# Gated linear recurrence and gated unit: when GpSimd issues the transfers of two weight matrices

## The chip, the cores and the metric

The kernel runs on one core of a Trainium2 chip. A core has five engines that each work through a queue of their own in order: PE (matrix multiplies, transposes and, counted apart, weight loads), DVE (VectorE), ACT (ScalarE), POOL (GpSimd) and SP, which here only issues transfers. DMA engines, 16 to a core, move data between HBM and the on-chip memory; SP, ACT and POOL can hand them work. The metric is device time in microseconds for one execution; lower is better. Time before is the median of five executions.

## The reference

Inputs are x, r_gate and i_gate of 4 x 6336 x 256 float32, a vector a_param of 256, two 256 x 256 weight matrices (w_val, w_out) and a convolution kernel conv_w of 5 x 256. Cut to what is computed:

```python
log_a = 8 * sigmoid(r_gate) * log(clip(sigmoid(a_param), 1e-6, 1 - 1e-6))
a_t   = exp(log_a)
gated = sqrt(max(1 - a_t * a_t, 1e-6)) * sigmoid(i_gate) * x
h_t   = a_t[:, t] * h + gated[:, t]          # recurrence over t, y[:, t] = h_t
gate  = sigmoid(sum_k conv_w[k] * y[t - 4 + k])   # causal, five taps
out   = (gate * (y @ w_val)) @ w_out
```

The two weight matrices are needed only in the last line, after the recurrence.

## The kernel before

The 4 x 6336 time steps are laid out as one row of 25,344 and cut into tiles of 512 steps (three of them 256), and tiles into chunks: one of 256, one of 512, 23 of 1024 (two tiles each), then 512, 256, 256. The channels are two halves of 128. Numbers below count tiles (g), chunk halves (k = 2 x chunk + half), and pieces of 256 output rows (q).

Per tile or chunk half these steps run, named as in the code:

- SP loads a tile of both gates (`load`, line 262, into `ri`) and of x (`loadx`, line 269, into `xt`).
- ACT takes tanh of both gates (`tanh`, line 354). The sigmoid is written through tanh.
- PE transposes the r half to channels (`srT`, line 379), ACT takes exp to get a (`exp`, line 388, into `aring`), POOL squares a (`e`, line 396, into `ering`).
- For a group of chunks at once (`UNITS`, the first two groups have chunks 0 and 1, and chunk 2), ACT takes the square root (`sq`, line 400). It needs another activation table, so a table load of 1.28 us goes before it and another after it.
- DVE or POOL makes (1 + tanh) * x (`u2`, line 365 on DVE, lines 369 and 370 on POOL), PE transposes the root to rows (`nT`, line 410), DVE multiplies (`xg`, line 417), PE transposes the product to channels (`xT`, line 426).
- DVE runs the recurrence (`scan`, line 444, into `yring`), PE the convolution (`conv`, line 470), ACT its tanh (`tg`, line 478), PE the product with w_val (`val`, line 486), DVE the gating (`gv`, line 496), PE the product with w_out (`out`, line 508), DVE or ACT the copy out (`osb`), SP the store.

The order in which each engine takes its steps is written out by hand (`ORDER`, line 48), a letter for a step. ACT starts with tanh 0, exp 0, exp 1, tanh 1, exp 2, tanh 2, tanh 3, exp 3, 4 and 5, tanh 4, and then both roots; POOL starts with six squares, e 0 to e 5, and then u2 of tile 2. A planner (`make_plan`) merges the five orders by estimated start times into one list, `plan`, and the steps are emitted in that list's order. Each engine keeps its own order; semaphores do the rest.

Ahead of the plan stands a setup: the small vectors, the identity matrices, the ten diagonal matrices of the convolution (`diag`, line 323, on DVE), the first eight load steps on SP, and the weights. `wv` (line 288) and `wo` (line 294) are bfloat16 tiles on chip; the matrices in HBM are float32, and the transfer converts them. POOL issues these transfers: four for `wv` (line 292, one for each half of rows and of columns) and two for `wo` (line 296). In POOL's queue they stand behind the making of the identity matrix and ahead of e 0. The first readers are `val` of tile 0 and `out` of piece 0 on PE.

Of the kernel before, what the change touches and what calls it, by code (L numbers as in the profile page):

```python
# [9 lines left out]
P = 128  # L10
# [50 lines left out]
BANK_ORDER = ("2220300232032030101322321213031230312121301103230301320123103021230121321321012121032312030131032110"  # L61
              "3203210321303123021032021023120103120130231030231023013203121032031230131302102302031031220131201321"
              "03120202310233203213201203302132002310232320202312303203031210")
TABLE, SEM, DMA_LAT = 1.3, 0.15, 2.2
START, ACT_START = 0.9, 4.6
FP32 = mybir.dt.float32
# [158 lines left out]
def kernel(  # L225
# [11 lines left out]
    nc = tc.nc  # L237
    B, S, D = x.shape
    assert D == 2 * P, f"kernel assumes D == 256, got {D}"
    H = D // P  # L240
# [31 lines left out]
    with tc.manual_schedule():  # L272
# [13 lines left out]
        b025 = const.tile([P, 1], FP32, name="b025")  # L286
        nc.vector.memset(b025[:], 0.25)
        wv = const.tile([P, H, D], BF16, name="wv")

        for hk in range(H):  # L290
            for m in range(H):
                nc.gpsimd.dma_start(wv[:, hk, m * P:(m + 1) * P].rearrange("p (h c) -> p h c", h=H),
                                    moe_w_val[hk * P:(hk + 1) * P, :].rearrange("p (h m c) -> p m h c", h=H, m=2)[:, m])
        wo = const.tile([P, H, D], BF16, name="wo")
        for h in range(H):
            nc.gpsimd.dma_start(wo[64 * h:64 * h + 64, :, :],
                                moe_w_out[h * P:(h + 1) * P, :].rearrange("(m c) n -> c m n", m=2))
        khf = const.tile([P, H], FP32, name="khf")
        wcol = const.tile([P, H, CONV_K], FP32, name="wcol")
        with tc.tile_pool(name="ps_setup", bufs=1, space=bass.MemoryType.PSUM) as ps_setup:  # L300
# [222 lines left out]
        def op_store(g, eng):  # L523
# [2 lines left out]
            nc.sync.dma_start(of[t0:t0 + nt, :].rearrange("(p j) d -> p j d", j=nj),  # L526
                              live.pop(("osb", g))[:, 0:nj, :])

        ops_by_name = dict(load=op_load, loadx=op_loadx, tanh=op_tanh, u2=op_u2, srT=op_srT, exp=op_exp, e=op_e, sq=op_sq,
                           nT=op_nT, xg=op_xg, xT=op_xT, scan=op_scan, conv=op_conv, tg=op_tg, val=op_val, gv=op_gv,  # L530
                           out=op_out, osb=op_osb, store=op_store)
        for (t, op, i, eng, dur) in plan:
            ops_by_name[op](i, eng)


# [28 lines left out]
```

## Time and profile before

| | before |
|---|---|
| median of five executions | 313.71 us (311.72 to 314.97) |
| the profiled execution | 314.52 us, of it 312.7 us span from the first instruction to the last |
| busy ACT | 284.5 us (91% of the span) |
| busy DVE | 269.7 us (86%) |
| busy PE | 252.1 us (81%); weight loads 163.3 us (52%) |
| busy POOL | 245.3 us (78%) |
| moved by DMA | 104.51 MB in 30,797 packets, 334 GB/s over the span |
| mean granted PE clock | 0.965 |

How to read it: no engine is busy all the time, and the largest share, ACT's, leaves 28 us of the span idle. A step's price is therefore not its busy time; it is what it adds to the chain of waits that ends last. The page's slices cut the span in 40 parts of 7.8 us. The timeline lists instructions by start time with, in brackets, the idle time of the engine before them and what ended it. A transfer issued by POOL shows on POOL's row for as long as GpSimd prepares it; the data lands later.

### The profile page before, as it was taken

What the parts mean: (1) busy time and instruction counts of PE and PEld (TensorE: products, weight loads), DVE (VectorE), ACT (ScalarE), POOL (GpSimd) and SP (SyncE); (2) the same over time, 40 slices, a digit from 0 to 9 for tenths busy, and PEclk for the clock granted to TensorE, in tenths of its full rate; (3) what the DMA queues carried; (4) which work ended last, traced back from release to release, by engine and by line L of the source; (5) the groups of instructions that cost most, each with busy time, mean ns of one, the idle gap of its engine ahead of it and who ended that gap; (6) DMA issues with size and microseconds to landing.
All of it is one profiled execution on the core that took longest, in us unless ns stands there. A gap on an engine that the chain in (4) does not pass through costs nothing.

```text
span 312.7 us, 6602 instructions
## 1 busy us (share of the span) xinstructions
PE 252.1 (81%) x2591; PEld 163.3 (52%) x2591; DVE 269.7 (86%) x273; ACT 284.5 (91%) x224; POOL 245.3 (78%) x154
## 2 busy tenths in 40 slices
PE   1226765887799987996897889979899989999994
PEld 1114533554565654655654565647555755666562
DVE  3015898698999989999799899999999999998983
ACT  5899898599999999999999979999999999989544
POOL 6273699859998997899999989998997987986000
PEclk9999987799999998899899899999999999999998
DMA  8999999996999699999994999999979979843345
GB/s 239 357 403 410 411 408 308 392 330 205 373 417 412 280 326 415 419 358 374 421 413 170 335 418 414 374 376 389 414 245 376 414 301 310 321 138 159 136 192 214
DMA packets 30797, 104.51 MB, mean 334 GB/s; under 512 B 4391, under 2 KB 4654, under 8 KB 30766
## 3 DMA queue, kind: packets, MB, share of 16 engines
q1 hardware_dynamic: 29376, 103.82, 87.2%
q0 software_dynamic: 1376, 0.26, 1.0%
q8 instruction: 20, 0.33, 0.4%
q14 instruction: 11, 0.09, 0.1%
q10 hardware_dynamic: 14, 0.01, 0.0%
HBM read 78.39 MB, written 25.95 MB: 334 GB/s over the span
## 4 chain that ended last, share of the span: by engine, by line
ACT 27%; DVE 25%; PE 22%; issue 13%; DMA 9%; SPq 3%; DVEq 0%; ACTq 0%
ACT tring L354 10%; DVE yring L444 10%; DMA ri<-in_i_gate_dram 9%; PE gp L470 6%; ACT ering L400 6%; ACT aring L388 5%; DVE osb L519 5%; DVE gv L496 4%; PE bank L410 4%; PE val L486 4%; PE bank L508 4%; ACT tg L478 3%; DVE uring L365 3%; DVE uring L417 3%; PE bank L426 3%
## 5 line engine op out<-in xcount | busy, mean ns | idle before, releaser
L396 POOL TENSOR_TENSOR ering<-aring 128x1024 f32<-128x1024 f32 (+2 forms) x56 | 95.5, 1720 | 34.9 <-ACT aring L388 34.9
L444 DVE TENSOR_TENSOR_SCAN yring<-aring,yring,bank 128x1024 bf16<-128x1024 f32 (+5 forms) x54 | 110.4, 2054 | 3.8 <-PE bank L426 3.7
L370 POOL TENSOR_TENSOR uring<-t,xt 128x1024 bf16<-128x1024 f32 (+1 forms) x43 | 101.1, 2350 | 4.2 <-DMA xt<-in_x_dram 0.7
L354 ACT ACTIVATE tring<-ri 128x2048 bf16<-128x2048 f32 (+1 forms) x51 | 94.3, 1865 | 0.8 <-DMA ri<-in_i_gate_dram 0.6
L470 PE MATMUL gp<-yring,diag 64*64 64x512 bf16 (+15 forms) x1196 | 68.7, 358 | 5.1 <-ACT tg L478 4.7
L388 ACT ACTIVATE aring<-bank,khf 128x1024 f32<-128x1024 bf16 (+2 forms) x56 | 61.0, 1113 | 9.8 <-PE bank L379 9.2
L508 PE MATMUL bank<-wo,gv 128*128 128x256 bf16 x396 | 58.2, 276 | 11.1 <-DVE osb L519 4.2
L496 DVE SCALAR_TENSOR_TENSOR gv<-tg,val 128x1024 bf16<-128x1024 bf16 (+1 forms) x54 | 60.6, 1127 | 6.2 <-PE val L486 4.3
L478 ACT ACTIVATE tg<-gp 128x1024 bf16<-128x1024 f32 (+1 forms) x51 | 51.2, 1004 | 8.9 <-PE gp L470 8.3
L486 PE MATMUL val<-yring,wv 128*128 128x512 bf16 (+1 forms) x204 | 52.8, 382 | 0.9 <-DVE gv L496 0.8
L508 PEld LDWEIGHTS <-gv 128*128 128x128 bf16 x396 | 37.1, 99 | 31.1 <-issue 16.9
L519 DVE TENSOR_SCALAR osb<-bank 128x512 f32<-128x512 f32 x74 | 48.8, 680 | 2.6 <-PE bank L508 2.1
L379 PE MATMUL bank<-ident_b,tring 128*128 128x128 bf16 x396 | 34.9, 235 | 17.4 <-ACT tring L354 11.2
L470 PEld LDWEIGHTS <-diag 64*64 64x64 bf16 x1196 | 31.2, 110 | 30.7 <-issue 16.2
L369 POOL TENSOR_SCALAR t<-tring 128x1024 f32<-128x1024 bf16 (+1 forms) x43 | 45.1, 1048 | 2.0
L400 ACT ACTIVATE ering<-ering,b 128x2048 bf16<-128x2048 f32 (+3 forms) x15 | 46.3, 3108 | 0.1
L410 PE MATMUL bank<-ident_f,ering 128*128 128x128 f32 x198 | 35.2, 309 | 12.6 <-ACT ering L400 8.0
L379 PEld LDWEIGHTS <-tring 128*128 128x128 bf16 x396 | 28.4, 105 | 25.9 <-ACT tring L354 13.2
L417 DVE TENSOR_TENSOR uring<-bank,uring 128x1024 bf16<-128x1024 bf16 (+1 forms) x51 | 33.3, 666 | 7.1 <-PE bank L410 6.9
L426 PE MATMUL bank<-ident_f,uring 128*128 128x128 f32 x198 | 33.5, 292 | 6.3 <-DVE uring L417 4.6
L410 PEld LDWEIGHTS bank<-ident_f,ering 128*128 128x128 f32 x198 | 28.2, 207 | 19.8 <-ACT ering L400 10.7
L365 DVE SCALAR_TENSOR_TENSOR uring<-tring,xt 128x512 bf16<-128x512 bf16 x15 | 20.0, 1378 | 15.1 <-DMA xt<-in_x_dram 15.1
(32 smaller groups left out, 104.5 us busy)
## 6 DMA issues: line engine op xcount, KB each, us to landing
ri<-in_r_gate_dram SPq DMA_DIRECT2D x48, 512.0 KB, 8.7
ri<-in_i_gate_dram SPq DMA_DIRECT2D x48, 512.0 KB, 9.6
xt<-in_x_dram SPq DMA_DIRECT2D x48, 512.0 KB, 9.2
out_dram<-osb SPq DMA_DIRECT2D x48, 512.0 KB, 5.0
ri<-in_r_gate_dram SPq DMA_DIRECT2D x3, 256.0 KB, 5.5
ri<-in_i_gate_dram SPq DMA_DIRECT2D x3, 256.0 KB, 5.5
xt<-in_x_dram SPq DMA_DIRECT2D x3, 256.0 KB, 4.5
out_dram<-osb SPq DMA_DIRECT2D x3, 256.0 KB, 2.4
```

Of the source, the lines that this page charges most:

```text
L354: nc.scalar.activation(out=tring[:, r:i + 1:i - r, 0:nj, :], in_=ri[:, :, 0:nj, :], func=ACT.Tanh, scale=0.5)
L370: nc.gpsimd.tensor_tensor(out=u.rearrange("p w d e -> p w e d"), in0=t1.rearrange("p (w e) d -> p w e d", e=2), in1=xt.rearrange("p (w e) ...
L388: nc.scalar.activation(out=aring[:, h, a0:a0 + nt].rearrange("c (w p j) -> c w p j", p=P, j=nj), in_=live.pop(("srT", k))[:, 0:nt].rearran ...
L396: nc.gpsimd.tensor_tensor(out=ering[:, H * e0 + h * nt:H * e0 + (h + 1) * nt], in0=a, in1=a, op=ALU.mult)
L400: nc.scalar.activation(out=nring[:, 2 * H * e0:2 * H * e0 + H * m], in_=ering[:, H * e0:H * (e0 + m)], func=ACT.Sqrt, scale=-0.25, bias=b0 ...
L410: nc.tensor.transpose(out=nT[:, w * D + h * P:w * D + (h + 1) * P], in_=ering[:, n0 + w:n0 + nw * P:nw], identity=ident_f[:])
L444: nc.vector.tensor_tensor_scan(out=yring[:, h, y0 + c0:y0 + c1], data0=aring[:, h, a0 + c0:a0 + c1], data1=xT[:, c0:c1], initial=0.0 if fr ...
L470: nc.tensor.matmul(out=gp[64 * h:64 * h + 64, m, c0:c1], lhsT=diag[rows, h, kk, rows], rhs=yring[rows, h, src:src + c1 - c0], start=(sh == 0),
L486: nc.tensor.matmul(out=val[:, m, 0:nt], lhsT=wv[:, hk, m * P:(m + 1) * P], rhs=yring[:, hk, y0:y0 + nt], start=(hk == 0), stop=(hk == H - 1))
L496: nc.vector.scalar_tensor_tensor(out=gv[:, 0:nj, hs, :].rearrange("c j h p -> c j (h p)"), in0=tg[:, hs, 0:nt].rearrange("c h (p j) -> c j ...
L508: nc.tensor.matmul(out=ops[:, e * D:(e + 1) * D], lhsT=gv[:, 2 * i + e, hk, :], rhs=wo[:, hk, :], start=(hk == 0), stop=(hk == H - 1))
L519: nc.vector.tensor_scalar(out=dst, in0=ops[:], scalar1=0.5, scalar2=None, op0=ALU.mult)
```

## The change

The two loops that issue the six weight transfers move from the setup into a function, and the loop over the plan calls it once, right after it has emitted step ("e", 1). In POOL's queue the six transfers then stand between e 1 and e 2. Their sizes, shapes and order among themselves stay, the tiles `wv` and `wo` stay where they were allocated, and every other instruction keeps its place on its engine and its waits.

```diff
+WEIGHTS_AFTER = ("e", 1)
...
         wv = const.tile([P, H, D], BF16, name="wv")
-
-        for hk in range(H):
-            for m in range(H):
-                nc.gpsimd.dma_start(wv[:, hk, m * P:(m + 1) * P].rearrange("p (h c) -> p h c", h=H),
-                                    moe_w_val[hk * P:(hk + 1) * P, :].rearrange("p (h m c) -> p m h c", h=H, m=2)[:, m])
         wo = const.tile([P, H, D], BF16, name="wo")
-        for h in range(H):
-            nc.gpsimd.dma_start(wo[64 * h:64 * h + 64, :, :],
-                                moe_w_out[h * P:(h + 1) * P, :].rearrange("(m c) n -> c m n", m=2))
...
+        def load_weights():
+
+            for hk in range(H):
+                for m in range(H):
+                    nc.gpsimd.dma_start(wv[:, hk, m * P:(m + 1) * P].rearrange("p (h c) -> p h c", h=H),
+                                        moe_w_val[hk * P:(hk + 1) * P, :].rearrange("p (h m c) -> p m h c", h=H, m=2)[:, m])
+            for h in range(H):
+                nc.gpsimd.dma_start(wo[64 * h:64 * h + 64, :, :],
+                                    moe_w_out[h * P:(h + 1) * P, :].rearrange("(m c) n -> c m n", m=2))
...
         for (t, op, i, eng, dur) in plan:
             ops_by_name[op](i, eng)
+            if (op, i) == WEIGHTS_AFTER:
+                load_weights()
```

## The prediction

> **What bounds the kernel now.** I read the page's slices first. They show that the DMA engines are full from about 8 us to 47 us; the compute engines take turns.
>
> ```profile
> DMA  8999999996999699999994999999979979843345
> q0 software_dynamic: 1376, 0.26, 1.0%
> ACT 27%; DVE 25%; PE 22%; issue 13%; DMA 9%; SPq 3%; DVEq 0%; ACTq 0%
> ```
>
> The second line is the queue that GpSimd feeds, which only the weights use. Its 1376 packets carry 0.26 MB, a four-hundredth of all bytes, and yet take 1.0% of the 16 engines' time, that is 0.010 x 312.7 = 3.1 us of the whole DMA system. The third line says that the chain which ended last is spread over ACT, DVE and PE. Of its 9% DMA, the chain in order of time shows where the first stretch lies:
>
> ```profile
> 4.26 9.85 DMA ri<-in_i_gate_dram
> 14.17 0.04 issue
> 14.21 1.92 ACT tring L354
> ...
> 19.02 1.90 ACT tring L354
> 20.94 0.97 ACT L400
> 21.98 0.25 issue
> 22.23 1.59 ACT ering L400
> ```
>
> The start is one chain: the fourth tile's gates land, then tanh 3, exp, tanh 4, a table load and the first root. ACT's own timeline tells what that landing costs:
>
> ```profile
> 11.68 1.90 ACT L354 ACTIVATE tring<-ri 128x2048 bf16<-128x2048 f32 x1
> 14.21 1.91 ACT L354 ACTIVATE tring<-ri 128x2048 bf16<-128x2048 f32 x1 [0.63 <-DMA ri<-in_i_gate_dram]
> 16.03 3.10 ACT L388 ACTIVATE aring<-bank,khf 128x512 f32<-128x512 bf16 x3
> ```
>
> Tanh 2 ends at 13.58 and tanh 3 starts at 14.21. That 0.63 us is the only time in the whole span that line 354 sat idle for a transfer of `ri`. POOL's timeline of the same stretch:
>
> ```profile
> 1.46 3.06 POOL L292 DMA_DIRECT2D wv<-in_moe_w_val_dram  x4
> 4.51 1.20 POOL L296 DMA_DIRECT2D wo<-in_moe_w_out_dram  x2
> 7.56 0.61 POOL L396 TENSOR_TENSOR ering<-aring 128x256 f32<-128x256 f32 x1 [1.85 <-ACT aring L388]
> 8.58 0.61 POOL L396 TENSOR_TENSOR ering<-aring 128x256 f32<-128x256 f32 x1 [0.41 <-ACT aring L388]
> 11.86 1.04 POOL L396 TENSOR_TENSOR ering<-aring 128x512 f32<-128x512 f32 x1 [2.67 <-ACT aring L388]
> 16.87 1.04 POOL L396 TENSOR_TENSOR ering<-aring 128x512 f32<-128x512 f32 x1 [3.97 <-ACT aring L388]
> 18.11 3.74 POOL L396 TENSOR_TENSOR ering<-aring 128x1024 f32<-128x1024 f32 x2 [0.20 <-ACT aring L388]
> ```
>
> POOL has holes of 2.67 and 3.97 us around e 2. Last, busy time by stretch (the last column is GB/s moved) and the weights' own rows:
>
> ```profile
> 4.00:18.00 14.00, 4.03 (x28) 2.65 (x28) 2.99 (x13) 11.60 (x12) 5.01 (x7) 1.00 1.12 348
> 18.00:36.00 18.00, 9.13 (x66) 6.63 (x67) 10.14 (x14) 16.58 (x13) 9.64 (x5) 1.00 1.03 412
> ```
>
> ```profile
> L486 PE MATMUL val<-yring,wv x204: 272/379/634, 35.9 to 307.1; 128*128 128x512 bf16 x96, 128*128 128x256 bf16 x6
> DMA to landing us min/median/max: 6.1/9.2/11.6
> ```
>
> The rate is 348 GB/s while the weights travel and 412 GB/s behind them. `wv` is first read at 35.9 us; the same view of `wo` gives a landing of at most 13.6 us after issue and a first reader at 40.1 us.
>
> **Removed from the start.** The six issues took POOL from 1.46 to 5.71, 4.25 us. POOL then waited 1.85 us for exp 0 anyway, and exp 0 hangs on tanh 0, which starts at 5.32 right behind a table load of 1.28 us that no transfer moves. So emptying POOL there is worth nothing. What is worth something is the rate. Views by 2 us give 311, 311, 351, 371 and 348 GB/s from 4 to 14. Against 412 that is 101 + 101 + 61 + 41 + 64 = 368 GB/s, times 2 us = 0.74 MB, or 1.8 us at 412. Without weights the gates of tile 3, ready at 14.11 (4.26 + 9.85), would be ready near 12.3.
>
> **Added behind e 1.** e 1 ends at 9.19; six issues at the old price end at 13.44. Their first packets reach the DMA engines a little later: in the rate, the fall came about 2.5 us after the first issue, so from some 11.7 on. From there to 13 the old loss of 64 GB/s costs 0.1 to 0.3 us, so tile 3 is ready at about 12.6, a full microsecond ahead of tanh 2's end at 13.58. Tanh 3 then starts at 13.58: **gain 0.63 us**, and no more, since ACT is the next limit. The same holds for tanh 1 and tanh 2, which start (8.40, 11.68) with no idle time for a transfer, so they gain nothing.
>
> **What stands behind the six issues on POOL.** e 2 could start at 11.86 and now starts at 13.44, 1.6 us late, and ends at 14.48. Only the first root, at 22.23, reads it, together with e 3. e 3 waits for exp 3: 16.87 now, 16.24 with the gain, so 1.8 us of the hole is left and the delay dies there. At nothing, covered by the hole of 3.97 us. If it were not covered: e 3, e 4, e 5 and the second root (23.8, behind the first of 1.59 us) have about 2 us more, e 5 ending at 21.85. The point from which it costs is six issues of over 16.87 - 1.04 - 9.19 = 6.6 us to move e 3, and over 8.6 us to move a root. The rows bound the issues at 6 x 0.60 = 3.6 us (shortest row) and 6 x 0.91 = 5.5 us (longest): nothing in either case. I take 4.25 us, the same six instructions.
>
> A stretched issue is what a rule speaks for. Where VectorE works beside it, the row at hand is `wo`: its two issues at 4.51 to 5.71 lay under the ten DVE instructions of line 323 (4.32 to 6.37, 2.05 us busy) and took 604 and 613 ns, no longer than the `wv` issues of 713 ns. The Trainium skill, SBUF — State Buffer, section "SBUF: two separate sides", says that some VectorE instructions lock GpSimd out of a shared port so that it can't write transfer descriptors, and gives some 620 ns alone against 3100 ns beside a copy; by that the six would take an estimated 18.6 us and e 2 would start near 27.8, some 10 us past what a root can bear. In the new place the trace shows DVE idle from 6.4 to 15.1 (it waits 8.8 us for `xt`), so I keep the row.
>
> **Where the rate goes.** The 3.1 us of DMA time are not saved, they move from about 4 to 18 us to about 12 to 26 us. Loads issued by 14 us land earlier, those behind 26 us at the same byte count as before. In between: DVE's u2 of tile 1 waits for `xt` until 22.18 and POOL's u2 of tile 2 until 23.51. With a trough as long as the old one, 14 us from 12 on, two thirds to three quarters of the moved packets lie ahead of these two points, so of 3.1 us some 0.8 to 1.0 us are still in their favour, a little over the 0.63 that they need to keep step with ACT. If not, u2 of tile 2 (ends 26.25) is read by `xg` only at 31.36. At nothing. The weights land by 13.44 + 13.6 = 27.0 (`wo`) and 12.3 + 11.6 = 23.9 (`wv`), so 13 and 12 us ahead of their readers: no wait added. The Trainium skill, DMA: Bandwidth & Descriptors, section "Rules for kernel authors", advises issuing a transfer early and waiting on it late; by that alone the sum would be zero or a loss, while the row shows that early issue bought a wait for tile 3.
>
> **What is late next.** From 14.21 to 42 the chain is a string of ACT, PE and DVE steps without a transfer, so the shift passes through undiminished; the next DMA stretches lie at 135 us (6.5 us) and 233 us (11.3 us), both for loads that SP issued just before, so they shift along. Sum: -0.63 us, bounded by 0 (it is swallowed) and -0.63. Against the profiled execution: 314.52 - 0.63 = 313.9. That execution stands 0.81 over the median of the runs, so for the median 313.71 - 0.63 = **313.1 us**.
>
> **The rivals.** *Swallowed:* the DMA engines are full until 47 us, and the bytes up to there are the same; a step bound by landing would take the 0.63 back, giving 313.7. Against it: between 26 and 42 us the chain has no DMA piece. *Slower, the issues stretch:* line 365 on DVE, a row that meets POOL's work, runs 0.69 us at best and 2.86 at worst, 4.1 times. Six issues so stretched take 17.6 us, 9 us past the 8.6 from which a root moves: 323. Against it: DVE's hole from 6.4 to 15.1. *Other meetings of DVE and POOL:* line 365's 15 instructions sum to 20.0 us where 15 x 0.69 would be 10.4; a shifted start could undo a third of those 9.6 us, or add one: 310.5 or 316.9. Against it: all engines shift alike. That the change does not do what it says is excluded by the instruction lists, which differ in that move alone.
>
> **How the numbers follow.** Forecast 0.63, swallowed 0.22, stretched issues 0.05, better meetings 0.07, worse 0.03. The first two both lie within 1% (3.1 us, about what a measurement of this kernel can tell from no change, the five runs being 3.25 us wide); they make 0.85. Faster is 0.07, slower 0.08. The range: 313.1 to 313.7, widened by about half of the runs' spread below the median (2.0) and above (1.3), less than a median of five would usually stray; it reaches from 311.2 to 314.8, and holds both likely cases.
>
> **What would show it.** Right: POOL's six issues at 9.2 to 13.5 taking 4.2 us in sum, e 2 at 13.4 and e 3 still waiting for ACT; 400 GB/s or more from 4 to 10 us and the trough of 350 from about 12 to 26; tanh 3 at 13.6 with no idle time; the first root at 21.6; the first `val` near 35.2, with no wait for a transfer. Wrong: issues over 1.1 us each, a root that waits for POOL, a PE wait for `wv` or `wo`, or the first root at 21.6 but the 100 us mark of the chain unmoved (swallowed).

## The result and the profile after

| | before | after |
|---|---|---|
| median of the executions | 314.39 us (311.22 to 318.29, 95 executions) | 313.27 us (309.47 to 316.46, 53 executions) |
| ratio after / before | | 0.9955, 95% interval 0.9939 to 0.9970 |
| profiled execution, span | 312.7 us | 312.7 us |
| first root starts (profiled execution) | 22.23 us | 21.45 us |

The kernel is faster by 0.45%, 1.4 us of 314.4, with an interval of 0.9 to 1.9 us. Ratios, here and below, leave out executions over 1.5% above the fastest of the same kernel in a series (here 19 of the 54 of the changed kernel, its profiled one among them; 14 of the 35 of the kernel before in the series of the holds, of no weights and of behind e 5), so plain means over all executions stand beside some of them. Here these are 313.32 and 314.60, 1.3 us apart (54 and 95 executions). The two profiled executions have the same span, so the gain can't be read from the spans; it has to be read from the start, and then followed.

ACT's timeline of the changed kernel answers to the one of before:

```profile
11.63 3.71 ACT L348 ACTIVATE tring<-ri 128x2048 bf16<-128x2048 f32 x2
...
21.45 3.47 ACT L394 ACTIVATE ering<-ering,b 128x1536 bf16<-128x1536 f32 x2
```

Tanh 2 and tanh 3 are now one row of 3.71 us from 11.63 on, without idle time between them: the 0.63 us wait for the gates of tile 3 is gone. The first root starts 0.78 us earlier. Of that, 0.12 us lies ahead of tanh 0 (5.20 against 5.32; a step that scatters, 5.51 in the repeat below) and 0.63 us is the wait. POOL's timeline of the same stretch:

```profile
9.02 3.05 POOL L527 DMA_DIRECT2D wv<-in_moe_w_val_dram  x4
12.07 1.21 POOL L530 DMA_DIRECT2D wo<-in_moe_w_out_dram  x2
13.27 1.08 POOL L390 TENSOR_TENSOR ering<-aring 128x512 f32<-128x512 f32 x1
16.08 1.04 POOL L390 TENSOR_TENSOR ering<-aring 128x512 f32<-128x512 f32 x1 [1.74 <-ACT aring L382]
```

The six issues take 4.26 us, as they did at the start, and e 2 stands behind them from 13.27 on. e 3 still waits 1.74 us for ACT; the delay of e 2 died in that hole. Busy time by stretch (the last column is GB/s):

```profile
4.00:6.00 2.00, 0.00 (x0) 0.00 (x0) 1.96 (x12) 1.99 (x2) 0.00 (x0) 1.00 0.78 283
6.00:12.00 6.00, 1.80 (x12) 1.11 (x12) 0.24 (x2) 4.30 (x6) 4.15 (x6) 1.00 1.01 404
12.00:28.00 16.00, 5.18 (x26) 3.13 (x26) 5.10 (x7) 15.91 (x11) 10.80 (x9) 1.00 1.12 373
28.00:36.00 8.00, 5.73 (x59) 4.31 (x58) 6.71 (x7) 7.03 (x7) 2.62 (x2) 1.00 1.03 418
```

The trough of the transfer rate has moved from 4 to 18 us to 12 to 28 us, where it costs 373 against 418 GB/s. From 6 to 12 us the rate is 404. But from 4 to 6 us it is 283 GB/s although no weight is on its way, so the weights alone don't account for the slow start. The page's slices, the weights' queue and the shares of the chain that ended last:

```profile
DMA  7999999886999889999995999999979989843345
...
q0 software_dynamic: 1376, 0.26, 1.0%
...
DVE 30%; ACT 22%; PE 22%; issue 14%; DMA 7%; SPq 2%; DVEq 0%; ACTq 0%
```

The weights still take 1.0% of the 16 DMA engines, so nothing was saved there; it was only moved. The chain that ended last has less ACT in it and more DVE. Why the gain is not in this execution's span shows further on, in DVE's timeline:

```profile
31.18 4.24 DVE L359 SCALAR_TENSOR_TENSOR uring<-tring,xt 128x512 bf16<-128x512 bf16 x4
35.34 1.27 DVE L438 TENSOR_TENSOR_SCAN yring<-aring,yring,bank 128x512 bf16<-128x512 f32 x1
```

and on POOL:

```profile
32.67 2.19 POOL L390 TENSOR_TENSOR ering<-aring 128x1024 f32<-128x1024 f32 x1 [7.21 <-ACT aring L382]
```

The row of 31.18 is DVE's u2 of tiles 3 and 4, four instructions. In the kernel before they took 2.53 us:

```profile
31.97 2.53 DVE L365 SCALAR_TENSOR_TENSOR uring<-tring,xt 128x512 bf16<-128x512 bf16 x4
34.42 1.28 DVE L444 TENSOR_TENSOR_SCAN yring<-aring,yring,bank 128x512 bf16<-128x512 f32 x1
```

In the changed kernel's execution e 6 began on POOL at 32.67, ahead of the fourth u2 instruction, which then took 2.41 us and ended only after e 6 did. The scan begins at 35.34 instead of 34.42: the start's 0.78 us are gone at this point, and 0.92 us more. e 6 came early because exp 6 did (9.94 us behind the first root, against 10.34 before), and PE had run the 16 transposes ahead of it in 1.24 instead of 1.91 us.

The prediction named a sign for a gain that is swallowed: the first root near 21.6, but the 100 us mark of the chain unmoved. From the chain that ended last, first the kernel before:

```profile
100.28 2.40 DVE yring L444 x2
```

and the changed kernel:

```profile
101.22 2.40 DVE yring L438 x2
```

The same two scans start 0.94 us later, not earlier. In this execution the lead of the start is lost by 35 us, and it isn't back at 100 us.

### The profile page after: what moved, and what is told of

It is laid out like the page before. It is cut to its first block, busy times and chain, and to the rows that moved or that the text cites. A ratio compares the mean times of both kernels' runs of the same rounds, so it can differ in the third digit from the quotient of the medians.

```text
span 312.7 us, 6602 instructions
## 1 busy us (share of the span) xinstructions
PE 249.4 (80%) x2591; PEld 162.0 (52%) x2591; DVE 271.6 (87%) x273; ACT 284.6 (91%) x224; POOL 245.1 (78%) x154
## 4 chain that ended last, share of the span: by engine, by line
DVE 30%; ACT 22%; PE 22%; issue 14%; DMA 7%; SPq 2%; DVEq 0%; ACTq 0%
DVE yring L438 11%; ACT tring L348 9%; PE gp L464 6%; DVE osb L513 6%; DVE gv L490 5%; PE bank L502 4%; ACT aring L382 4%; DVE uring L359 4%; PE val L480 4%; ACT ering L394 4%; DVE uring L411 3%; PE bank L404 3%; DMA ri<-in_r_gate_dram 3%; ACT tg L472 3%; PE bank L420 3%
## 5 line engine op out<-in xcount | busy, mean ns | idle before, releaser
L464 PE MATMUL gp<-yring,diag 64*64 64x512 bf16 (+15 forms) x1196 | 67.4, 353 | 4.8 <-ACT tg L472 4.4
L480 PE MATMUL val<-yring,wv 128*128 128x512 bf16 (+1 forms) x204 | 52.0, 378 | 1.4 <-DVE gv L490 1.2
L373 PE MATMUL bank<-ident_b,tring 128*128 128x128 bf16 x396 | 34.1, 231 | 15.9 <-ACT tring L348 10.6
L404 PEld LDWEIGHTS bank<-ident_f,ering 128*128 128x128 f32 x198 | 28.2, 207 | 21.6 <-ACT ering L394 9.2
L359 DVE SCALAR_TENSOR_TENSOR uring<-tring,xt 128x512 bf16<-128x512 bf16 x15 | 22.3, 1530 | 14.3 <-DMA xt<-in_x_dram 14.3
```

Source lines behind the costliest of these rows:

```text
L373: nc.tensor.transpose(out=srT[:, col:col + P], in_=tring[:, g % NTR, j, h * P:(h + 1) * P], identity=ident_b[:])
L404: nc.tensor.transpose(out=nT[:, w * D + h * P:w * D + (h + 1) * P], in_=ering[:, n0 + w:n0 + nw * P:nw], identity=ident_f[:])
L464: nc.tensor.matmul(out=gp[64 * h:64 * h + 64, m, c0:c1], lhsT=diag[rows, h, kk, rows], rhs=yring[rows, h, src:src + c1 - c0], start=(sh == 0),
L480: nc.tensor.matmul(out=val[:, m, 0:nt], lhsT=wv[:, hk, m * P:(m + 1) * P], rhs=yring[:, hk, y0:y0 + nt], start=(hk == 0), stop=(hk == H - 1))
```

## The experiments

All ratios are against the kernel before on the same chip. Twelve executions of each kernel and 35 of before give intervals of 0.8 to 1.4 us to each side, so most of the weight lies on the profiles' first 40 us, and the times are read for sign and rough size.

### The start, held back by hand

One idle ACT instruction on the changed kernel, two longer ones on the kernel before, both directly ahead of tanh 3:

```diff
+        idle = const.tile([P, 1024], BF16, name="idle")
...
             ri = live.pop(("ri", g))
+            if g == 3:
+                for _ in range(1):
+                    nc.scalar.activation(out=idle[:, 0:512],
+                                         in_=diag[:].rearrange("p h k c -> p (h k c)")[:, 0:512], func=ACT.Tanh, scale=0.5)
```

> The changed kernel with one idle ACT instruction (128x512, about 0.6 us) directly ahead of tanh 3. Theory (the whole gain is the time at which tanh 3 starts): tanh 3 is back at 14.0 to 14.2, the first root at 22.0 to 22.3, and the time goes back to that of before, ratio 0.998 to 1.002. Rival (the gain has another source, such as what POOL and DVE meet later): the ratio stays near 0.9955.

> The kernel before with two idle ACT instructions (128x1024 each, about 2.0 us in sum) directly ahead of tanh 3. They start at 13.6, so 0.63 us of them lie under the wait for the gates, and tanh 3 moves from 14.2 to about 15.6. Theory (a shift of the start passes through to the end one for one): +1.4 us, ratio 1.003 to 1.007. Rival (a shift of the start is swallowed by slack further on): ratio 0.998 to 1.002. Rival (a shift of the start is amplified, since what POOL and DVE meet changes): +3 us or more, ratio over 1.009.

Measured: the changed kernel, held, 313.77 us, ratio 0.9998 (0.9964 to 1.0032). The kernel before, held, 315.88 us, ratio 1.0053 (1.0021 to 1.0086). ACT's timelines, first the changed kernel, held:

```profile
14.09 0.62 ACT L350 ACTIVATE idle<-diag 128x512 bf16<-128x512 bf16 x1
14.61 1.90 ACT L353 ACTIVATE tring<-ri 128x2048 bf16<-128x2048 f32 x1
```

and the kernel before, held:

```profile
14.27 2.13 ACT L356 ACTIVATE idle<-diag 128x1024 bf16<-128x1024 bf16 x2
16.31 1.89 ACT L359 ACTIVATE tring<-ri 128x2048 bf16<-128x2048 f32 x1
```

Both ratios lie in the theory's ranges, but only the second carries weight. Its first root, at 24.31, is 1.4 us behind the mean of the five profiles of the kernel before that stand in the table below, and the time went up by 1.7 us by the ratio, 1.5 by the plain means: in the kernel before, a shift of the start reaches the end about one for one. The first neither shows that the gain is gone nor that it is left: its interval doesn't exclude a gain of 1.1 us, its plain mean is 0.4 us under before's, and giving 0.62 us back could undo only part of a gain of 1.1 to 1.4. Both profiles missed their expected times by 0.4 to 0.7 us, in the same way: tanh 1 had waited for its gates, 0.59 us in one and 0.69 us in the other.

### No weight transfers at all

```diff
+        nc.gpsimd.memset(wv[:], 0.0625)
+        nc.gpsimd.memset(wo[:], 0.0625)
...
-            if (op, i) == WEIGHTS_AFTER:
-                load_weights()
```

> Leaves out the six weight transfers; POOL fills wv and wo with a constant instead, ahead of its first square. Theory (the gain is tanh 3's wait for its gates, which the weights' packets cause at the start, and ACT is the next limit): the early part is that of the changed kernel, tanh 3 at 13.4 to 13.6 with no idle time and the first root at 21.4 to 21.6, and the time is that of the changed kernel, ratio to before 0.993 to 0.998. Rival (the packets still cost in their new place, from 12 to 28 us, or 3.1 us of DMA time count wherever they are): clearly faster than the changed kernel, ratio 0.985 to 0.992. Rival (the gain comes from somewhere later): no statement on tanh 3.

This kernel leaves out the six transfers and fills both tiles with a constant; it is run for its times alone. Measured: 313.50 us, ratio 1.0028 (0.9983 to 1.0072), plain mean 0.8 us under before's. The ratio lies above the expected 0.993 to 0.998; by the plain means (0.9975) it would lie inside, so the size of the gain is not to be had from this run. Either way it is not faster than the changed kernel: in their new place the 3.1 us of DMA time cost nothing that can be measured, and the rival that counts them wherever they are is out. ACT's timeline:

```profile
9.18 1.91 ACT L350 ACTIVATE tring<-ri 128x2048 bf16<-128x2048 f32 x1 [0.80 <-DMA ri<-in_i_gate_dram]
...
12.47 3.78 ACT L350 ACTIVATE tring<-ri 128x2048 bf16<-128x2048 f32 x2
```

Tanh 3 follows tanh 2 without idle time, as expected (the row of 3.78 us holds both). But tanh 1 waited 0.80 us for its gates with no weight packet in the machine, so tanh 3 started at 14.34 and the first root at 22.36, both later than expected and the root no earlier than in the first profile of the kernel before. So a part of tanh 1's wait is not the weights' doing.

### Other places for the transfers

```diff
-WEIGHTS_AFTER = ("e", 1)
+WEIGHTS_AFTER = ("e", 3)
```

and, in the other kernel, ("e", 5).

> The six transfers stand behind e 3 in POOL's queue. Theory (the prediction's point from which the issues cost): e 3 ends near 17.1, the issues end near 21.4, e 4 and e 5 end near 25.2, and the second root, which could start near 23.0, waits for POOL until then, so the root ends about 2.1 us late; against the changed kernel +2 us, ratio to before 1.001 to 1.006. Rival (POOL's delay dies in slack further on): ratio as the changed kernel's, 0.994 to 0.998.

> The six transfers stand behind e 5 in POOL's queue instead of behind e 1: issued at about 21 to 25.3 us, ahead of u2 of tile 2. Theory (only the packets ahead of tanh 3 cost; the first reader of wv at 34.7 us sets the latest issue): the early part as in the changed kernel up to the first root; val of tile 0 waits for wv by 0 to 2 us (last wv issue near 23.6 plus a landing of 10 to 13 us); u2 of tile 2 on POOL moves from 25.5 to about 29, still ahead of its reader at 30.6; ratio to before 0.995 to 1.002. Rival (a later place is a better place, because the gates of tiles 4 and 5 land earlier too): faster than the changed kernel, ratio under 0.993.

Measured: behind e 3, 314.10 us, ratio 1.0018 (0.9984 to 1.0052). ACT's timeline:

```profile
25.90 2.00 ACT L394 ACTIVATE ering<-ering,b 128x2048 bf16<-128x2048 f32 x1 [2.09 <-POOL ering L390]
```

The second root waited 2.09 us for POOL, where 2.1 had been worked out, and the time went up by about that against the changed kernel (0.9938 in the same series). This is the prediction's point from which the issues cost, made to happen, and it shows where the room ends: POOL's hole ahead of e 3 is the last one ahead of the roots that can hold the issues.

Behind e 5, 315.20 us, ratio 1.0011 (0.9965 to 1.0056), so the rival of a still better place (under 0.993) is out. POOL's and PE's timelines:

```profile
20.94 3.06 POOL L527 DMA_DIRECT2D wv<-in_moe_w_val_dram  x4
24.00 1.21 POOL L530 DMA_DIRECT2D wo<-in_moe_w_out_dram  x2
```

```profile
36.63 0.28 PE L480 MATMUL val<-yring,wv 128*128 128x256 bf16 x1 [1.13 <-DMA wv<-in_moe_w_val_dram]
```

`val` of tile 0 stood 1.13 us in the middle of its four matmuls until the last piece of `wv` had landed, inside the 0 to 2 us expected; so transfers can also be issued too late. The six issues here ran beside 2.12 us of DVE work (u2, xg and the first scans) and took the 4.26 us of the other places. The rule of the Trainium skill weighed in the prediction (SBUF — State Buffer, "SBUF: two separate sides": some VectorE instructions keep GpSimd from writing descriptors) is not seen for these DVE instructions; whether they are of the kind that the page means, no run here shows.

### Only half of the transfers moved

The two transfers of `wo` move behind e 1, the four of `wv` stay ahead of all.

> Only the two transfers of wo move behind e 1; the four of wv (1024 of the 1280 data packets) stay ahead of all. Theory (the packets that travel ahead of tile 3's gates are what costs): the rate from 4 to 12 us is as before, 310 to 370 GB/s, tanh 3 waits for its gates until 13.9 to 14.2, or is held by a late tanh 1 to the same time; ratio 0.998 to 1.002. Rival (what counts is that POOL is free early, or the number of transfers ahead): part of the gain, ratio near 0.997.

Measured: 313.89 us, ratio 1.0012 (0.9969 to 1.0055). ACT's timeline:

```profile
9.57 1.91 ACT L353 ACTIVATE tring<-ri 128x2048 bf16<-128x2048 f32 x1 [1.08 <-DMA ri<-in_i_gate_dram]
...
15.21 1.91 ACT L353 ACTIVATE tring<-ri 128x2048 bf16<-128x2048 f32 x1 [0.45 <-DMA ri<-in_i_gate_dram]
```

No gain, as the theory has it: with `wv`'s packets at the start the rate from 6 to 12 us was 356 GB/s (344 before, 404 in the changed kernel; over all profiles 344 to 365 in the seven with `wv` ahead and 375 to 412 in the seven without). The tanh 3 row is the important one. Tanh 1 had waited 1.08 us and tanh 3 waited again, 0.45 us, so the two waits add up, and the first root came at 23.23, 1 us later than in the profile on which the prediction rests.

### The changed kernel once more, and further profiles of the kernel before

> The changed kernel once more, beside this chip's runs of the kernel before. If the gain is the 0.63 to 0.78 us by which the profile shows the first root earlier: ratio near 0.9975. If the measured 1.4 us is the true size and something further on adds to it: ratio near 0.9955. Where tanh 1 waits 0.6 to 0.8 us for its gates (three of six profiles so far), the first root lies near 22.2; where it does not, near 21.4.

> The kernel before, unchanged, for another profile of its start. Seven profiles with the weights' packets behind tile 1's gates put the first root at 21.39 to 22.36 us (that of after_hold less its 0.62 us of idle work), mean 21.9; the spread comes from tanh 1, which waits 0 to 0.8 us for its gates. Theory (the packets ahead of tile 1's and tile 3's gates delay both, so the change gains more than 0.78 us on average): in four more profiles of the kernel before, tanh 1 waits in most, tanh 3 waits again behind it, the first root lies at 22.2 to 23.3, mean 22.7 or more. Rival (tanh 1's wait is chance and hides tanh 3's): the first root lies at 22.2 to 22.5 in all, mean gain 0.3 to 0.5 us.

The other profiles of the kernel before have the same expectation in short:

> As before_look1: first root at 22.2 to 23.3 by the theory, at 22.2 to 22.5 by the rival.

Measured: the changed kernel 312.59 us, ratio 0.9938 (0.9904 to 0.9972), first root at 21.68. Its upper end is a gain of 0.9 us, so 0.63 or 0.78 is not the whole of it. But the four u2 instructions took 4.24 us again, the scan behind them came 13.91 us after the first root (13.89 in the first profile, 12.17 to 12.19 in all five of the kernel before), and the scans of the 100 us mark started at 100.35. The five profiles of the kernel before have them at 99.37 to 102.02, 100.62 on average. So of a lead of 1.4 and 1.2 us at the first root (22.88 on average before), none and 0.3 us are left at 100 us in the changed kernel's two profiles. The profiled executions of the kernel before took 312.97, 314.21, 317.30 and 312.20 us. ACT's timeline in the first:

```profile
8.39 1.90 ACT L354 ACTIVATE tring<-ri 128x2048 bf16<-128x2048 f32 x1
...
14.12 1.91 ACT L354 ACTIVATE tring<-ri 128x2048 bf16<-128x2048 f32 x1 [0.55 <-DMA ri<-in_i_gate_dram]
```

and in the second:

```profile
10.20 1.91 ACT L354 ACTIVATE tring<-ri 128x2048 bf16<-128x2048 f32 x1 [1.70 <-DMA ri<-in_i_gate_dram]
...
15.86 1.91 ACT L354 ACTIVATE tring<-ri 128x2048 bf16<-128x2048 f32 x1 [0.47 <-DMA ri<-in_i_gate_dram]
```

The first is like the profile on which the prediction rests: tanh 1 unhindered, tanh 3 waiting 0.55 us, root at 22.14. In the second, tanh 1 waited 1.70 us and tanh 3 another 0.47, and the root came at 23.88. The third is like the second (1.28, 0.48, root at 23.87), the fourth like the first (0, 0.53, root at 22.29). Put together:

| kernels | tanh 1 waits, us | tanh 3 waits, us | first root, us |
|---|---|---|---|
| before, five profiles | 0, 0, 0, 1.28, 1.70 | 0.63, 0.55, 0.53, 0.48, 0.47 | 22.23, 22.14, 22.29, 23.87, 23.88; mean 22.88 |
| only `wo` moved, one profile | 1.08 | 0.45 | 23.23 |
| weights behind e 1, four profiles | 0, 0, 0.51, 0.59 | 0 in all | 21.45, 21.68, 22.06, 22.00 (held kernel, less its 0.62); mean 21.80 |
| no weights, behind e 3, behind e 5 | 0.80, 0.37, 0 | 0 in all | 22.36, 22.23, 21.39 |

Tanh 3 waited in all six of these profiles that have `wv` ahead of it, and in none of the six others in which no idle work stands ahead of it: this wait is the weights' doing. The first roots of the kernel before and of the one with the weights behind e 1 differ by 1.1 us on average, against the 0.9 to 1.9 us of the measured times. In "most" profiles tanh 1 was expected to wait, and it did in two of four; but tanh 3 waited behind it every time, the mean of the four roots is 23.05, and the rival's 22.2 to 22.5 in all is out. The roots spread wider than the theory's 22.2 to 23.3.

### The meeting of DVE and POOL at 32 us

```diff
+        seen = const.tile([P, 2], BF16, name="seen")
...
             a = aring[:, h, a0:a0 + nt]
+            if k == 6:
+                nc.gpsimd.tensor_copy(out=seen[:], in_=uring[:, 4 % NU, 512:514])
```

> The changed kernel with one tiny POOL copy ahead of e 6 that reads the last output of DVE's u2 of tile 4, so that e 6 can't start before that instruction has ended. In the changed kernel's profile this DVE instruction, begun at 33.0 us, took 2.41 us beside e 6 where 0.69 is its time alone, and DVE's next scan began at 35.34 where a uniform shift of 0.79 would have put it at 33.6. Theory (this meeting takes back in some executions what the start gains): u2 of tiles 3 and 4 take 2.5 us in sum, the scan starts within 2.6 us of u2's start, e 6 starts at 33.0 to 33.9; ratio 0.990 to 0.996, under the changed kernel's. Rival (the delay of e 6 costs as much on ACT, or the meeting just moves to the next pair): ratio as the changed kernel's.

Measured: 313.05 us (312.62 to 314.10), ratio 0.9969 (0.9944 to 0.9993). In its profile the four u2 instructions took 2.53 us, as they should, e 6 began at 34.52, later than the expected 33.0 to 33.9, and the 100 us mark came at 99.50. The expected gain over the changed kernel did not show: the medians of the changed kernel are 313.27 and 312.59. So that the meeting, which costs 1.7 us where it happens, reaches the end is not shown. What changed is the spread. The 12 executions lie within 1.5 us, those of the changed kernel beside it within 5.2 us (310.67 to 315.82). This fits a copy that fixes the order of an otherwise open meeting, at the price of the good outcomes along with the bad ones, but 12 executions and one profile don't prove that; it was not tried on the kernel before.

## Why the prediction was right, and where it was short

- **The chain at the start**: right up to the first root. Tanh 3 waits for its gates in the profiles with `wv` ahead and not in those without, and the root comes earlier. That "the shift passes through undiminished" is shown only for the kernel before, by the hold; in both profiles of the changed kernel the lead is lost by 36 us, and at most 0.3 us of it is there at 100 us.
- **Six issues behind e 1, 4.25 us, hidden by POOL's holes**: right to the hundredth (4.26; e 2 at 13.27 against 13.44; e 3 still waiting 1.74 against 1.8). The point from which they cost was right in kind too: behind e 3, where the hole is gone, a root waits 2.09 us.
- **The weights land ahead of their readers**: right; the first `val` ran at 34.7 without a wait, and behind e 5 it waited.
- **The trough moves and costs nothing in its new place**: right; without any transfers the kernel is no faster. The rate of 400 GB/s from 4 us on was wrong for 4 to 6 us (283), which cost tanh 3 nothing.
- **Swallowed**: as a forecast of no gain it is out, by the interval and by the repeat, and its case, loads that land late until 47 us, was not seen: behind 20 us the only waits for a load up to 110 us are those for `xt`, 6.3 and 0.7 us before and after. (The changed kernel's chain does pass through a load of x from 89.75 on, 6.91 us, which the chain of before has not; but DVE, where it ends, shows no idle time there.) But the sign that the prediction set for it, an early root with the 100 us mark unmoved, is there in both profiles. Which way the 1.4 us reach the end is not shown.
- **The size, -0.63 us**: too small; measured 0.9 to 1.9 us. The step that most likely fell short is the term of the sum which says that tanh 1 and tanh 2 "start (8.40, 11.68) with no idle time for a transfer, so they gain nothing". That was true of the one profile at hand. In five profiles of the kernel before, tanh 1 waited 0, 0, 0, 1.28 and 1.70 us, and with the weights moved 0 to 0.59. The wait of tanh 3 comes on top each time. At the first root the difference was 1.1 us in place of 0.63, by five profiles against four. That the forecast time, 313.1, lies 0.2 us from the measured 313.27 is luck: the base, 313.71 from five executions, was 0.7 us under the later 314.39, and the gain was too small by about as much.
- **Other meetings of DVE and POOL**: held a true mechanism at too low a rank. Such a meeting took 1.7 us of u2 time in the profiled execution of the changed kernel, and again in its repeat (4.24 us for the four instructions), and in none of five profiles of the kernel before. "All engines shift alike" failed there: PE's transposes were 0.67 us shorter, so exp 6 and with it e 6 moved more than DVE did.
- **Readings and sums**: the slices shown have nines up to 70 us; 47 us is where the page's GB/s fall, from 408 to 308. The 20.0 us of line 365 is the time in which one of its instructions ran; their sum is 20.7. The range is said to be widened by about half of the spread (2.0 and 1.3), but 311.2 and 314.8 lie 1.9 and 1.1 us outside, nearly the whole of it.

What stays open: how the gain gets from the first root to the end; why the gates of tile 1 land at such different times (0.80 us of wait occurred with no weights at all), and how much of its spread the weights cause. Five profiles against four put the added wait near 0.3 us (0.60 against 0.28 on average), but they scatter by 1.7, so the term blamed above is likely and not shown. Whether the difference between 1.1 us at the first root and 1.4 us at the end is anything but spread can't be told either.

## What to carry to other kernels

Transfers that are needed late and consist of many small packets may be better issued behind the first large loads, and into a hole of the issuing engine that the trace shows; by the Trainium skill's advice alone (DMA: Bandwidth & Descriptors, "Rules for kernel authors": issue early, wait late) they would have stayed first, and here 0.26 MB at the front cost about 1 us at the first root. One profile shows one outcome of a race: where a step starts just after its input lands, take several profiles before writing that it doesn't wait. And compare a small gain at a marker early in the chain, since times of single executions of this kernel scatter by more than 5 us, and at later ones too: here the lead at 22 us was gone at 36.

## What the runs showed of the hardware that was not expected

Time goes with the granted PE clock: over 54 recorded executions of the changed kernel the correlation of time with mean granted clock (0.964 to 0.987) is -0.73, about half of the spread, and 0.005 less clock goes with some 0.8 us. And the first microseconds of loading are uneven on their own: in the seven profiles without weights on the way the rate from 4 to 6 us was 246 to 377 GB/s, against 387 to 426 between 8 and 12 us.
